# Token lists of the expert units built by small TensorE products instead of a scatter through DRAM; router constants built in steps; zeros of the output written later

## The chip, the core and the metric

The kernel runs on one core of a Trainium2 chip. The metric is device time in microseconds (us); lower is better. TensorE (PE), VectorE (DVE), ScalarE (ACT), GpSimd (POOL) and SyncE (SP, which only issues transfers here) each run their own queue in order; an instruction at the head of a queue holds everything behind it until the semaphores that it waits for are set.

## What is computed

Four batches of 576 tokens go through attention over 32 memories per head, then a gated MLP (512 to 1536 to 512), then a mixture of 8 experts with one expert per token and a capacity.

```python
a = exp(phi - max(phi, axis=2)); a /= sum(a, axis=2)            # per batch and head
k_m, v_m = einsum('bhsm,bhsd->bhmd', a, k), einsum('bhsm,bhsd->bhmd', a, v)
x = softmax(q @ k_m.T / 8) @ v_m                                # 2304 tokens x 512
x = (silu(x @ w_gate) * (x @ w_val)) @ w_out                    # 512 -> 1536 -> 512
expert = argmax(x @ moe2_w_gate); gate_w = softmax(...)[expert] # 8 experts
# tokens of an expert in order, at most `capacity`; others give 0
out[i] = gate_w[i] * (relu(x[i] @ w1[expert]) @ w2[expert])     # 512 -> 1024 -> 512
```

## The kernel before

All large products are float32 in three passes over rounded high and low parts (each operand is cut once: the high part by ACT at L370, the low part by DVE or POOL at L372). Weights arrive in 128x512 pieces, are turned by one ACT and three DVE instructions (L676 to L682), cut, used for the tokens of pass 1, stored to DRAM (`wsc`, `osc`) and loaded again at L730 for pass 2, which takes the second 1152 tokens.

Per batch, attention makes the memories (`kvp`, `tv`, L478 to L534) and the scores `at`; `pm` (L761) folds the memories into the gate and value weights, cut into `mh`; `pg` and `pv` (L863) are the gate and value products, 128x288 each; ACT makes `sg` (L773), DVE multiplies (L776), and the cut result `gh` enters `py` (L907, the MLP's output), summed over three groups G of the hidden width. Where the last group is done, `rows_out` adds up the rows (`rows`, L945), `store_rows` writes them to the DRAM tensor `x2` (L982), PE turns them (`pw`, L956) and multiplies by the router's weights `rg` (`pl`, L966).

`route` runs once for each of 6 blocks of 384 tokens. From the logits it finds each token's expert and its position in the expert's list (DVE instructions of 24 elements or less, four small PE products L1050 to L1054), and writes the token numbers with three indirect DMAs (L280, POOL) to the list tensor `perm` in DRAM. `weigh` stores the gate weights beside the rows (`gr`, L1115). `unit_table` turns the counts into units of 288 list places: two early ones, taken after pass 1's tokens, and six late ones. `unit_slots` lets SP read each unit's first place into a register and loads its 288 numbers (`idx`, L1212); `usable` makes `idg` of them (L1223, L1225). A unit then gathers its rows from `x2` (`xr`, L1301, POOL), turns them (`pxt`, L1324), multiplies by its expert's weights (`p`, L1351 and L1391), turns back (`po`, L1417) and scatters to the output (L280).

`routing_tables` builds the router's constants (`tri`, `rev`, `capf`, `thr`, `rg` and others) in one go: after batch 1's attention is done, all its instructions stand in one row on each engine, with three transfers (`cap_i`, `perm`, `rg32`). Then `tables` issues 18 writes of zeros to `x2` (second half) and 18 to the output (L1605).

What stands where in each engine's queue is settled when the kernel is built. A planner (`Loom`) steps through the work as threads: of those that could start on the engine that is free first it takes the one with the lowest rank (the table `RANK` shifts ranks), by assumed costs of each instruction (`on_v`, `on_a`, `on_pe`, `on_dma`). The result is a fixed order; nothing is moved at run time.

Of the kernel before, what the change touches and what calls it, by code (L numbers as in the profile page):

```python
# [20 lines left out]
RANK = {  # L21
    "gate": -9.6, "mh": 21.5, "mem": -52.9, "mem0": -65.1, "py": 200.6, "out": 236.4, "tables": 237.0, "warm": -9,
# [5 lines left out]
    "py1": 18.8, "turn": -10.4, "route": -70.2, "zeros": 4.5, "lists": -31.0, "reload": 13.3, "w1": 79.0, "w2": 46.2,  # L28
    "gather": 179.4, "x": 62.0, "up": 31.6, "hidden": -83.6, "down": 7.4,
    "l": (120.7, -0.9, 139.8, 37.0, 32.1, 45.2, 46.4, 56.0, 62.2, 66.5, 80.1, 63.5, 98.2, 102.9, 183.0, 198.1, 201.7, 200.6),  # L30
    "w": (-35.1, 193.1, 24.8, 183.1, 35.8, 36.6, -20.5, 2.0, 176.1, 45.2, 213.9, 197.4, 173.3, 173.5, -36.9, 103.7, 192.5, 95.3),
# [18 lines left out]
class Loom:  # L50
# [5 lines left out]
    def __init__(self, slack=0.0):  # L56
        self.slack, self.table = slack, AF.Exp
# [62 lines left out]

    def run(self):
        while self.ready:
            start, _, th = min(((max(t.time, self.busy[t.want[0]]), t.rank, t) for t in self.ready), key=lambda x: x[:2])
            start += self.slack
            th = min(
                (t for t in self.ready if t.want[0] == th.want[0] and max(t.time, self.busy[t.want[0]]) <= start),
                key=lambda t: (t.rank, max(t.time, self.busy[t.want[0]])),
# [4 lines left out]
            start = max(th.time, self.busy[engine])  # L132
# [7 lines left out]
            else:  # L140
# [3 lines left out]
                if engine == "V" and len(th.want) > 2 and self.busy["G"] > start:  # L144
                    cost += 0.45 * min(cost / 0.55, self.busy["G"] - start)
# [35 lines left out]
def on_swdge():  # L181
    return "G", 0.95


SWDGE_LANDING = 2.5
# [3 lines left out]
def attention_moe_moe_kernel(  # L189
# [35 lines left out]
    PADBASE = E * NT  # L225
    NPERM = 128 * ((PADBASE + NB + 127) // 128)
# [71 lines left out]
    onesb = tri = rev_i = rev = tokid = cap_i = capf = ej_i = ejf = thr = unit_val = trib = uio_i = uio = x2 = perm = mark = carry = cnt = rg = zero = undone = None  # L298

    def routing_tables():  # L300
        nonlocal onesb, tri, rev_i, rev, tokid, cap_i, capf, ej_i, ejf, thr, unit_val, trib, uio_i, uio, x2, perm, mark, carry, cnt, rg, zero, undone
        onesb = sb.tile([128, 128], BF16, name="onesb")
        nc.vector.memset(onesb, 1.0)
        tri = sb.tile([128, 128], BF16, name="tri")
        nc.gpsimd.affine_select(tri, onesb, [[1, 128]], ALU.is_gt, 0.0, base=0, channel_multiplier=-1)
# [528 lines left out]
    def batch(b):  # L834
# [38 lines left out]
        loom.put(b_s)  # L873

    rows_stored = {k: Event() for k in range(2 * NTC)}
    early_gathered, pls, pl_left = Event(), {}, {}

    def products(P):

# [838 lines left out]
```

## Time and profile before

| | us |
|---|---|
| median of 3 runs | 725.56 (724.23 to 727.99) |
| profiled execution | 721.09 |
| its span | 719.1 |
| PE busy in it | 658.3 |

PE works 92% of the span, so the time is PE's work and the gaps in it. Idle time of other engines costs nothing unless PE waits for it. A row of the timeline gives start and length, engine, line, operation, tiles, the number of like instructions, and in brackets how long the engine had been idle and whose end let it go on.

### The profile page before, as it was taken

To read this page: it belongs to the slowest core of one execution; us is meant where nothing else is said; L and a number is where in the kernel's file an instruction comes from. 1 tells how busy PE (TensorE), PEld (TensorE's weight loads), DVE (VectorE), ACT (ScalarE), POOL (GpSimd) and SP (SyncE) were. 2 spreads that over 40 slices of the span, in tenths; PEclk is the share of its full clock that TensorE was granted. 3 is DMA by queue.
4 is the path that set the end of the run, shared out by engine and by line. 5 is a ranking of instruction groups with operands and counts; after the bars stand their busy time and mean duration, and the time that the engine had idled before them with its cause. 6 is when DMAs were issued, how large, how long until landed. Compare 5 with 4: busy or idle time off the path is not lost. (4 is left out here: it accounts for less than half of the span.)

```text
span 719.1 us, 12573 instructions
## 1 busy us (share of the span) xinstructions
PE 658.3 (92%) x4656; PEld 604.7 (84%) x4656; DVE 440.9 (61%) x890; ACT 364.2 (51%) x693; POOL 247.8 (34%) x232
## 2 busy tenths in 40 slices
PE   2599879999997998999999999998999999999893
PEld 2488669887886987898998998897999999999892
DVE  3799956479999754732444465761763754853633
ACT  3567647666577723744642552533454543643531
POOL 2175543435444603533221230223542531430302
PEclk9889989999999999999999999999999999999997
DMA  9877699996594536392420432604857845645431
GB/s 360 319 278 268 217 286 243 317 356 221 208 379 155 205 118 125 98 225 89 177 99 35 147 118 103 118 2 146 274 158 213 254 123 206 211 155 171 149 119 35
DMA packets 56224, 134.49 MB, mean 187 GB/s; under 512 B 10399, under 2 KB 24351, under 8 KB 51552
## 3 DMA queue, kind: packets, MB, share of 16 engines
q1 hardware_dynamic: 52352, 123.91, 54.1%
q0 software_dynamic: 3808, 9.75, 4.3%
q8 instruction: 38, 0.62, 0.4%
q14 instruction: 26, 0.21, 0.1%
HBM read 98.11 MB, written 35.79 MB: 186 GB/s over the span
## 5 line engine op out<-in xcount | busy, mean ns | idle before, releaser
L907 PE MATMUL py<-wo,gh 128*128 128x512 f32 x648 | 156.6, 393 | 0.8 <-POOL wo L372 0.8
L907 PEld LDWEIGHTS py<-wo,gh 128*128 128x128 f32 x648 | 118.9, 188 | 24.9 <-POOL wo L372 1.2
L372 POOL TENSOR_TENSOR gh<-sg,gh 128x288 fp32r<-128x288 f32 x96 | 84.3, 884 | 133.5 <-ACT gh L370 133.5
L1391 PE MATMUL p<-hh,w2h 128*128 128x288 f32 x768 | 115.6, 302 | 0.4 <-DVE xt L372 0.4
L1351 PE MATMUL p<-xt,w1h 128*128 128x288 f32 x768 | 112.6, 299 | 1.0 <-DVE ohb L1040 0.6
L1391 PEld LDWEIGHTS p<-hh,w2h 128*128 128x128 f32 x768 | 106.2, 191 | 1.0 <-DVE xt L372 0.6
L1351 PEld LDWEIGHTS p<-xt,w1h 128*128 128x128 f32 x768 | 105.4, 191 | 1.4 <-DVE ohb L1040 0.8
L863 PE MATMUL pg<-at,mh 128*128 128x288 f32 x576 | 97.3, 303 | 9.3 <-DVE mh L372 3.5
L863 PE MATMUL pv<-at,mh 128*128 128x288 f32 x576 | 93.3, 299 | 4.7 <-ACT sg L773 4.7
L863 PEld LDWEIGHTS pg<-at,mh 128*128 128x128 f32 x576 | 83.6, 191 | 16.6 <-DVE mh L372 5.7
L280 POOL DMA_INDIRECT out_dram<-ot,idx x24 | 48.9, 2038 | 134.7 <-DVE ot L1430 130.5
L863 PEld LDWEIGHTS pv<-at,mh 128*128 128x128 f32 x576 | 82.1, 190 | 5.9 <-ACT sg L773 5.0
L372 DVE TENSOR_TENSOR mh<-pm,mh 64x512 fp32r<-64x512 f32 (+1 forms) x88 | 60.3, 685 | 14.4 <-ACT mh L370 12.6
L776 DVE SCALAR_TENSOR_TENSOR sg<-sg,pv 128x288 f32<-128x288 f32 x96 | 42.5, 448 | 40.9 <-PE pv L863 24.5
L1365 ACT ACTIVATE hh<-p 128x288 fp32r<-128x288 f32 x64 | 26.2, 409 | 74.4 <-PE p L1351 72.2
L1367 DVE SCALAR_TENSOR_TENSOR hh<-p,hh 128x288 fp32r<-128x288 f32 x64 | 28.7, 450 | 53.4 <-ACT hh L1365 53.4
L370 ACT ACTIVATE gh<-sg 128x288 fp32r<-128x288 f32 x96 | 41.9, 442 | 36.4 <-DVE sg L776 35.5
L370 ACT ACTIVATE mh<-pm 64x512 fp32r<-64x512 f32 (+1 forms) x88 | 51.9, 590 | 13.2 <-PE pm L761 5.1
L372 DVE TENSOR_TENSOR w2h<-w2r,w2h 128x1024 fp32r<-128x1024 f32 x36 | 43.6, 1214 | 20.9 <-ACT w2h L370 20.9
L372 DVE TENSOR_TENSOR w1h<-w1r,w1h 128x1024 fp32r<-128x1024 f32 x36 | 43.1, 1219 | 20.9 <-PE pv L863 11.6
L761 PE MATMUL pm<-wgv,tv 128*128 128x256 f32 x336 | 48.5, 294 | 7.6 <-ACT wgv L370 6.0
L761 PEld LDWEIGHTS pm<-wgv,tv 128*128 128x128 f32 x336 | 45.1, 200 | 9.3 <-ACT wgv L370 6.3
(192 smaller groups left out, 839.8 us busy)
## 6 DMA issues: line engine op xcount, KB each, us to landing
w1r<-in_moe_w_dram SPq DMA_DIRECT2D x36, 512.0 KB, 4.8
w2r<-in_moe_w_dram SPq DMA_DIRECT2D x36, 512.0 KB, 5.2
wr<-in_moe_w_gv_dram SPq DMA_DIRECT2D x24, 512.0 KB, 6.4
wsc<-wgv SPq DMA_DIRECT2D x12, 1024.0 KB, 6.1
wgv<-wsc SPq DMA_DIRECT2D x12, 1024.0 KB, 7.1
kvraw<-in_kv_dram SPq DMA_DIRECT2D x16, 640.0 KB, 7.2
wr<-in_moe_w_out_dram SPq DMA_DIRECT2D x12, 512.0 KB, 6.6
osc<-wo SPq DMA_DIRECT2D x6, 1024.0 KB, 4.9
```

The lines of the kernel that those rows point to most:

```text
L280: ins = nc.gpsimd.indirect_dma_start(*args, **kwargs)
L370: nc.scalar.activation(hi, src, AF.Copy)
L372: (nc.gpsimd if pool else nc.vector).tensor_sub(lo, src, hi.bitcast(F32))
L761: nc.tensor.matmul(pm[:, Q * 256 : (Q + 1) * 256], tv[:, 2 * Q + hp, a, :], w[:, c, 2 * Q + hp], start=(k == 0 and n3 == 0), stop=(k == le ...
L776: nc.vector.scalar_tensor_tensor(sg, sg, 2.0**-16, pv[:, :NB], ALU.mult, ALU.mult)
L863: nc.tensor.matmul(pg[:, :NB], mh[:, a, Q, gv * 128 : gv * 128 + 128], at[:, Q, c, ns], start=(Q == 0 and n3 == 0), stop=(Q == 1 and n3 == 2),
L907: nc.tensor.matmul(py, gh[:, a, k * TC : (k + 1) * TC], wtiles[P, ws[j // 2]][:, j % 2, c, :], start=(j == 0 and n3 == 0), stop=(j == FG - ...
L1351: nc.tensor.matmul(p1[:, :NB], self.w1[d][:, a, f * 128 : f * 128 + 128], self.xt[d][:, c], start=(d == 0 and n3 == 0), stop=(d == NDT - 1 ...
L1365: nc.scalar.activation(dst[:, 0], p1[:, :NB], AF.Relu)
L1367: nc.vector.scalar_tensor_tensor(dst[:, 1], p1[:, :NB], 0.0, dst[:, 0].bitcast(F32), ALU.max, ALU.subtract)
L1391: nc.tensor.matmul(p2[:, :NB], self.w2[f // 2][:, f % 2, a, d * 128 : d * 128 + 128], self.hh[f][:, c], start=(f == 0 and n3 == 0), stop=( ...
```

## The change

Line numbers of the kernel after are higher: L372 is L429 there, L863 is L920, L907 is L964, L730 is L787, L1324 is L1453, L1351 is L1480, L1391 is L1520, L1417 is L1546, L1301 is L1432.

**Lists.** `perm`, its 18 scatters and the register reads are gone. `route` keeps for each token its place modulo 96 (`places`) and a group number for each third of a unit (`groups`). `marks` writes a 0/1 matrix `ones` (token by place) with one DVE comparison of 128x288 per block; `slots` writes `picked` (token by unit and third, times the token's number in two digits) with DVE, and sums ones x picked over 128-token blocks on PE: 9 products for the early units, 18 for the late ones. Six DVE instructions turn the sum into `idg` and `idx`. The last, small unit copies its column with four short transfers.

**Constants.** They are made in single steps from the moment that batch 0's scores start, each step ranked by the planner. **Zeros.** `x2` is not zeroed any more (early gathers read its first half only); the output's 18 zero writes wait until pass 2's first group has let go of its weights. **Planner.** New ranks throughout; transfers are not issued over 40 us ahead of the modelled DMA; POOL's work is charged to DVE where both run.

```diff
-    "gate": -9.6, "mh": 21.5, "mem": -52.9, "mem0": -65.1, "py": 200.6, "out": 236.4, "tables": 237.0, "warm": -9,
+    "gate": -427.7, "mh": -121.7, "mem": -6.5, "mem0": -3.9, "py": 225.9, "out": 216.2, "tables": 206.8, "warm": -9,
...
+    def tables():
...
+        yield atts[0].phq[0]
+        yield on_dma(20)
         nc.sync.dma_start(cap_i, capacity.bitcast(I32)[0:1].partition_broadcast(128))
+        yield on_dma(60)
+        nc.sync.dma_start(rg32, r_gate.rearrange("(t p) e -> p t e", p=128))
...
+            yield on_v(80)
+            nc.vector.tensor_copy(dst, src)
...
+    def zeros():
+
+        yield listed
+        yield wfree[1, (0,)]
+        for i in range(NT // 128):
+            yield on_dma(262)
+            nc.sync.dma_start(
...
@@ route @@
-        for c in range(RB):
-            yield on_swdge()
-            scatter(
-                "perm",
...
+        over = small([TC, RB, NQ - 1], "over", BF16)
+        yield on_v(69)
+        nc.vector.tensor_tensor(
...
+        nc.vector.tensor_reduce(q96, over, AX.X, ALU.add)
...
@@ lists @@
-        nc.sync.dma_start(idx[:, i], perm[bass.ds(first, NB)].rearrange("(p c) one -> p (c one)", c=NC))
...
+    def marks(key):
...
+        for blk in range(NBLK // 2 if early else NBLK):
             yield placed[blk]
+            yield on_v(RB * CH)
+            nc.vector.tensor_tensor(
+                t[:, blk * RB * CH : (blk + 1) * RB * CH].rearrange("p (t s) -> p t s", s=CH),
...
+    def slots(key, n, firsts, pk, left):
...
+        for a in range(2):
+            yield on_v(T * w)
+            nc.vector.tensor_tensor(
+                picked[:, :, a], picked[:, :, 1], number[:, :T, a : a + 1].to_broadcast([128, T, w]), ALU.mult
+            )
+        pt = pk[:CH, 128 : 128 + 2 * w]
+        yield on_pe(T, 100)
+        for i in range(T):
+            nc.tensor.matmul(
+                pt, ones[:, i], picked[:, i].rearrange("p a w -> p (a w)"), start=(i == 0), stop=(i == T - 1)
+            )
...
@@ tables @@
-        yield NEXT + RANK["zeros"]
-        for i in range(NT // 256, NT // 128):
-            yield on_dma(262)
-            nc.sync.dma_start(
-                x2[i * 128 : (i + 1) * 128, :DM].rearrange("p (t c) -> p t c", t=NDT),
-                zero.unsqueeze(1).to_broadcast([128, NDT, 128]),
-            )
...
```

SP at the start of the program, before (`wr` raw weights, `kvraw` keys and values, `ph` phi, `qt` queries):

```order
L439 DMA qt<-in_q_dram 128x1152 x2
L666 DMA wr<-in_moe_w_gv_dram 128x1024 x2
L416 DMA kvraw<-in_kv_dram 128x1280 x2
L396 DMA ph<-in_phi_dram 128x576 x2
L439 DMA qt<-in_q_dram 128x1152
L416 DMA kvraw<-in_kv_dram 128x1280 x2
```

And after:

```order
L723 DMA wr<-in_moe_w_gv_dram 128x1024 x2
L453 DMA ph<-in_phi_dram 128x576 x2
L473 DMA kvraw<-in_kv_dram 128x1280 x2
L496 DMA qt<-in_q_dram 128x1152
L453 DMA ph<-in_phi_dram 128x576 x2
L473 DMA kvraw<-in_kv_dram 128x1280 x2
```

Weights, phi and keys now come ahead of the queries; `cap_i` and `rg` (the router's weights) follow eight transfers later, ahead of the seventh piece of weights.

DVE where the constants are made, before (`wr` and `mag` are weights being turned, `sg` the gate times the value):

```order
L678 TENSOR_SCALAR wr_906<-mag_982 128x512
L494 RECIPROCAL rs_1026<-rs_1026 128x1
L303 MEMSET onesb_1066 128x128
L309 CAST rev_1072<-rev_i_1070 128x8
L315 CAST capf_1078<-cap_i_1076 128x1
L320 TENSOR_SCALAR ej_i_1080<-ej_i_1080 64x1
```

And after:

```order
L833 SCALAR_TENSOR_TENSOR sg_521<-sg_521,pv_504 128x288
L369 CAST shift_82<-ints_176 128x3
L429 TENSOR_TENSOR mh_522<-pm_442,mh_522 128x512
L369 CAST uio_89<-ints_176 64x16
L557 TENSOR_TENSOR kvs_529<-kvp_326,rh_513 128x2x2x64
L369 CAST capf_83<-cap_i_117 128x1
L739 SCALAR_TENSOR_TENSOR mag_456<-mag_456,wr_352 128x512
L833 SCALAR_TENSOR_TENSOR sg_550<-sg_550,pv_538 128x288
```

The 17 rows that stood together before are 22 single rows among the first gates' work now.

PE in the two early units, where the late lists are made, before (`hh` and `w2h`: second product, `y2` turned back):

```order
L1417 MATMUL po_5513<-ident_63,y2_5202 96x128
L1417 MATMUL po_5514<-ident_63,y2_5202 96x128
L1417 MATMUL po_5515<-ident_63,y2_5202 96x128
L1391 MATMUL p2_5556<-hh_5146,w2h_4702 128x288 x6
L1391 MATMUL p2_5556<-hh_5146,w2h_4752 128x288 x6
```

And after:

```order
L1546 MATMUL po_5469<-ident_63,y2_5187 96x128
L1546 MATMUL po_5470<-ident_63,y2_5187 96x128
L1546 MATMUL po_5471<-ident_63,y2_5187 96x128
L1520 MATMUL p2_5504<-hh_5130,w2h_4686 128x288 x6
L1520 MATMUL p2_5504<-hh_5130,w2h_4735 128x288 x6
L1318 LDWEIGHTS ones_5049
L1318 MATMUL pk_5381<-ones_5049 96x42
```

The 18 list products stand in a row there, each with its weight load; the first late gather's `pxt` comes 21 rows of large products behind the last of them.

## Rows read from the trace of the kernel before

**Rows 1.** Page, parts 1 and 2: busy time; granted clock in 40 slices.

```profile
PE 658.3 (92%) x4656; PEld 604.7 (84%) x4656; DVE 440.9 (61%) x890; ACT 364.2 (51%) x693; POOL 247.8 (34%) x232
...
PEclk9889989999999999999999999999999999999997
```

**Rows 2.** Waits of PE by line: us in total, times, longest us.

```profile
PE pg L863 <- DVE mh L372: 3.5, 4, 1.9
PE pxt L1324 <- DMA xr<-x,idg: 3.1, 3, 2.4
```

**Rows 3.** Stretches: busy PE, PEld, DVE, ACT, POOL, granted clock, DMA share, GB/s.

```profile
40.00:60.00 20.00, 19.91 (x196) 18.10 (x196) 19.69 (x36) 13.78 (x30) 14.82 (x13) 0.96 0.81 280
...
160.00:180.00 20.00, 17.82 (x97) 14.59 (x96) 19.84 (x32) 12.24 (x23) 11.56 (x10) 1.00 0.67 225
...
480.00:500.00 20.00, 18.18 (x138) 17.93 (x137) 2.29 (x7) 6.92 (x13) 3.57 (x4) 1.00 0.32 100
```

**Rows 4.** Timeline of PE at the start.

```profile
36.16 0.58 PE L761 MATMUL pm<-wgv,tv 128*128 128x256 f32 x1 [6.02 <-ACT wgv L370]
...
44.43 1.06 PE L863 MATMUL pg<-at,mh 128*128 128x288 f32 x6
```

**Rows 5.** Timeline, 94 to 112: PE, then ACT, DVE and SP.

```profile
105.67 1.81 PE L863 MATMUL pv<-at,mh 128*128 128x288 f32 x6 [4.72 <-ACT sg L773]
...
109.94 0.95 PE L863 MATMUL pv<-at,mh 128*128 128x288 f32 x6
...
104.60 0.22 ACT L357 CAST rg<-rg 128x32 fp32r<-128x32 f32 x1 [6.17 <-DMA rg<-in_moe_w_gate_dram]
...
104.08 0.15 DVE L315 CAST capf<-cap_i 128x1 f32<-128x1 int32 x1 [4.99 <-DMA cap_i<-in_moe_capacity_dram]
...
99.99 0.42 SPq L356 DMA_DIRECT2D rg<-in_moe_w_gate_dram  x1
```

**Rows 6.** Timeline, 278 to 290: PE, then DVE.

```profile
279.01 0.17 PE L1052 MATMUL pl<-ohb,onesb 128*128 128x16 bf16 x1
279.03 0.17 PE L1053 MATMUL pl<-ohb,onesb 128*128 128x8 bf16 x1
...
283.19 0.66 PE L956 MATMUL pw<-ident,rows 128*128 128x128 f32 x4 [2.44 <-DVE rows L945]
...
282.44 0.69 DVE L945 TENSOR_TENSOR rows<-py,yp 128x512 f32<-128x512 f32 x1 [4.02 <-DMA x<-rows]
```

**Rows 7.** Transfers of 262 to 290, then 420 to 458: KB, us to landing.

```profile
x<-rows SPq DMA_DIRECT2D x5, 256.0 KB, 8.9
...
perm<-tokid,addr POOLq DMA_INDIRECT x6, 12.0
x<-gr SPq DMA_DIRECT2D x2, 6.0 KB, 10.0
...
x<-rows SPq DMA_DIRECT2D x9, 256.0 KB, 2.3
```

**Rows 8.** Timeline, 470 to 506: PE, then DVE and SP.

```profile
475.78 3.48 PE L1391 MATMUL p<-hh,w2h 128*128 128x288 f32 x24
...
500.61 0.27 PE L1324 MATMUL pxt<-ident,xr 96*128 96x96 f32 x1 [2.43 <-DMA xr<-x,idg]
...
502.56 3.25 PE L1351 MATMUL p<-xt,w1h 128*128 128x288 f32 x12 [0.35 <-DVE hh L1367]
...
477.05 3.50 DVE L372 TENSOR_TENSOR w1h<-w1r,w1h 128x1024 fp32r<-128x1024 f32 x3
...
494.33 0.17 DVE L1223 TENSOR_SCALAR valid<-idx 96x18 f32<-96x18 int32 x1 [7.05 <-DMA idx<-perm]
...
486.34 5.73 SPq L1212 DMA_DIRECT2D idx<-perm  x6
```

**Rows 9.** Timeline of SP: zeros of the output; reloads of output weights.

```profile
128.62 12.62 SPq L1605 DMA_DIRECT2D out_dram<-zero  x13
...
395.56 4.43 SPq L730 DMA_DIRECT2D wo<-osc  x2
```

More of the change, by code (lines that the diff above doesn't have):

```diff
@@ L21 @@
 RANK = {
-    "gate": -9.6, "mh": 21.5, "mem": -52.9, "mem0": -65.1, "py": 200.6, "out": 236.4, "tables": 237.0, "warm": -9,
[5 rows of a table removed]
[L28 to L31, printed above, removed]
+    "gate": -427.7, "mh": -121.7, "mem": -6.5, "mem0": -3.9, "py": 225.9, "out": 216.2, "tables": 206.8, "warm": -9,
[5 rows of a table added]
+    "mh1": -125.4, "py1": 5.2, "turn": -32.0, "route": -35.0, "zeros": -96.4, "lists": -142.7, "marks": -35.9, "pick": 100.3,
[3 rows of a table added]
 }
@@ L119, in put, with earliest @@
             slots.free.append(self.now + self.hop())
+    def earliest(self, th):
+        time = max(th.time, self.busy[th.want[0]])
+        return max(time, self.busy["DMA"] - self.look) if th.want[0] == "SP" and len(th.want) == 2 else time
     def run(self):
         while self.ready:
-            start, _, th = min(((max(t.time, self.busy[t.want[0]]), t.rank, t) for t in self.ready), key=lambda x: x[:2])
+            start, _, th = min(((self.earliest(t), t.rank, t) for t in self.ready), key=lambda x: x[:2])
             start += self.slack
             th = min(
-                (t for t in self.ready if t.want[0] == th.want[0] and max(t.time, self.busy[t.want[0]]) <= start),
-                key=lambda t: (t.rank, max(t.time, self.busy[t.want[0]])),
+                (t for t in self.ready if t.want[0] == th.want[0] and self.earliest(t) <= start),
+                key=lambda t: (t.rank, self.earliest(t)),
             )
@@ L131, in run @@
             self.running = engine
-            start = max(th.time, self.busy[engine])
+            start = self.earliest(th)
             if engine == "SP" and len(th.want) > 2:
@@ L143, in run @@
                     cost += 1.3
-                if engine == "V" and len(th.want) > 2 and self.busy["G"] > start:
-                    cost += 0.45 * min(cost / 0.55, self.busy["G"] - start)
+                if engine == "V" and len(th.want) > 2:
+                    if self.busy["G"] > start:
+                        cost += 0.45 * min(cost / 0.55, self.busy["G"] - start)
+                    self.shared = start + cost
+                if engine == "G" and self.shared > start:
+                    self.busy["V"] += 0.45 * min(cost, self.shared - start)
                 self.busy[engine] = th.time = start + cost
@@ new lines, in tables @@
+        for dst, src in (
+            (place_of, parts[0]),
+            (steps, parts[1]),
+            (number[:, :, 0], parts[2]),
+            (number[:, :, 1], parts[3]),
+            (rev[:, 0, :], parts[4]),
+            (shift, parts[5]),
+            (uio, parts[6][:NEJ]),
+            (capf, cap_i),
+        ):
+            yield on_v(80)
+            nc.vector.tensor_copy(dst, src)
+        ej = ints[:NEJ, at : at + 2]
+        yield on_v(40)
+        nc.vector.tensor_scalar(ej[:, 0:1], parts[7][:NEJ], 3, None, ALU.arith_shift_right)
@@ L1190, in unit_table @@
[L1190 to L1193 removed]
+        nc.vector.tensor_copy(tab, tabf[:, 0:17])
         tabs[early] = tab
         loom.set(tab_ready[early], loom.now + 0.3)
[L1198 to L1202 removed]
+        if not early:
+            yield on_v(16)
+            nc.vector.tensor_copy(firstf, pk[:, 64:80])
@@ L1203, in unit_slots @@
+        left[0] -= 1
+        if not left[0]:
+            loom.put(banks)
+    idxs, idx_ready, turned_on = {}, {key: Event() for key in "eld"}, {}
+    marked = {key: Event() for key in "eld"}
+    def marks(key):
+        early = key == "e"
+        yield placed[0 if early else NBLK // 2]
+        yield raw_s
+        turned_on[key] = t = traw([128, 2560], "ones", BF16)
         for blk in range(NBLK // 2 if early else NBLK):
             yield placed[blk]
-        n, tab, key = len(us), tabs[early], "d" if dyn is not None else "e" if early else "l"
@@ L1469, in gather @@
             yield landed
[L1470 removed]
+            self.idx = idx
             yield self.prev.got
```

316 lines of the change are left out of this document (183 added, 133 removed), and 13 rows, old and new, of the table RANK.

## The prediction

> **What bounds the kernel now.** I read the busy times first. PE works 658.3 of 719.1 us [rows 1], so 60.8 us are gaps, and some work is stretched: the granted clock is 10 tenths in most slices, 7 to 9 in a few. I then took 20 us stretches one by one. Most of those after 300 us are full. In 40 to 60 and 160 to 180 VectorE is busy 19.69 and 19.84 of 20 us [rows 3], and the PE gaps there wait for `mh`, which VectorE cuts: 3.5 us over four waits [rows 2]. That part of the kernel is bound by VectorE's order, and small things put among its work count there. The list of waits by line then gives single long gaps, and the timeline at each of them tells who came last. Four concern the change.
>
> Start: `pm` waits 6.02 us for the cut of the first weights and the first `pg` starts at 44.43 [rows 4].
>
> Constants: VectorE and ScalarE both stand, 4.99 and 6.17 us, at the head of their queues, for `cap_i` and for `rg`, issued at 99.99; behind them stand a cut of `mh` and the gates. PE starts `pv` at 105.67 after 4.72 idle, and the six products then last 1.81 us instead of 0.95 [rows 5]: the clock has gone to half (1.2 of 2.4 GHz) after the gap.
>
> Rows: VectorE stands 4.02 us at `rows` for the store of older rows that must leave their buffer, and PE's `pw` comes 2.44 us late [rows 6].
>
> Lists: `valid` stands 7.05 us until SP has read the six lists back, issued from 486.34 on one behind another in 5.73 us; the gathers follow it, and `pxt` waits at 500.61 [rows 8], in three waits for 3.1 us in all [rows 2].
>
> **The change part by part**, against the profiled execution of 721.09 us.
>
> *Constants in steps.* The transfers go out behind the first weights and queries, tens of us before their first use. Both stalls go, and with them `pv`'s 4.72. From 105.67 to 109.94 stand 18 products (12 of 128x288, 6 of 128x256) in 4.27 us; at 0.145 or less each (24 in 3.48, [rows 8]) they take 2.6 at most, so 1.7 to 2 of clock go too. Together 6.6. What is late next there: the cut of `mh` and the gates that stood behind the two waits, and their inputs were ready. The instructions do not vanish: 22 small ones at about 0.15 [rows 5] are 3.3 us at most, less where they overlap the tails of others, and they now stand in VectorE's bound stretch after 40 us. Seventeen of them cost nothing before, being under the stall. I charge 1.5, between 0 and 3.3.
>
> *Start.* The queries go behind weights, phi and keys. The sixth weight piece still ends the wait for `pm`, but phi's sums and the keys' products are no longer behind the weights. Counting the VectorE work ahead of the first `pg` I expect it 2 to 4 us before 44.43; I take 3, less the 1.5 above: 1.5 net. The bounds are -2 and 4.5.
>
> *Scatters gone.* In 262 to 290 the six scatters took 12.0 us (median) from issue to landing, and stores of rows among them 8.9; with no scatters around, in 420 to 458, the same stores took 2.3 [rows 7]. With 2.3 the store that held `rows` would land over 6 us sooner, so the 4.02 go. PE gets back 2.44 and a clock dip. Its price I take from the dip after the lists: 12 products in 3.25 us instead of 1.74, so 1.5 [rows 8]. Together 3.9; bounds 0 and 3.9.
>
> The Trainium skill has a rule for this ("DMA: Bandwidth & Descriptors", section "Queues, rings and completion order"): a transfer's semaphore is a strongly ordered write that lands only after every earlier write from that engine, across its queues. By that rule a store that moves fast still signals late behind a slow scatter, which the 8.9 against 2.3 agrees with. It would hold as well behind the `gr` store, which stays: by that reading none of the 3.9 comes back.
>
> *Lists on chip.* The chain was: last scatter, its landing, six reads in turn, landing, `valid`, gather. Now it is VectorE and PE work. The route gets four more small instructions (0.6 us); the last mark of 128x288 costs 0.35, estimated from `w1h`'s 1.17 for 1024 columns [rows 8]; the picks of 18 blocks by 42 columns, by the same price per column, some 3.5; 18 products; four small instructions, 0.7. Three `w1h` cuts, 3.50, lie on the way [rows 8]. The choice of units is made some 3 us ahead of the cuts that start at 477.05 [rows 8]; from there the sum of these pieces ends at 484 to 487 instead of 494.5. VectorE has only 2.29 us of work in 480 to 500 [rows 3], so nothing else delays it. PE comes to the list products at an estimated 484.5 (by their place in the order, some 9 us of products behind 475.78 [rows 8]), so it may wait up to 2 us there; the gathers then land some 8 us sooner than before, against the 3.1 that they were late. Gone: 3.1, the following 0.35, and 1.5 of clock: 5.0. Bounds: 2 (a new wait of 2 us with a dip at the products) and 5.0.
>
> The products themselves: 27, each with a weight load of 128x96. The nearest rows are the router's bf16 products, 0.17 us long but 0.02 apart [rows 6]; with loads I take 0.06, so 1.6 us lost, bounds 0.5 and 4.6. The marks (nine at 0.35) and the extra route work (0.6 in each of six blocks) fall in 260 to 480, where VectorE is the waiting engine; PE's work covers them. If it did not, they would cost at most 6.8 together. GpSimd loses 18 scatters and SP its reads, and nobody waits for the gain beyond what is counted.
>
> *Zeros later.* In the old place nobody on PE waited for them. In the new one they stand on SP ahead of the reload of `wo` for the next group. Thirteen took SP 12.62 us [rows 9], so 18 take 17.5; a reload then needs 4.4 or so for two [rows 9] and lands perhaps 5 us after issue: 22 to 25 us. PE's cover, by the order of the kernel after, is 156 products of 128x288, 24 of 128x256 and six of 128x512 between the last use of the old tile and the first of the new: 25 to 27 us at 0.133 to 0.145 each. It just fits. I charge 0.5, bounds 0 and 4.5 (3 late and a dip).
>
> *New ranks.* Every order in the first 240 us is another one. The stretches of 20 us from 40 to 240, of which two have 0.09 and 2.18 us of gap [rows 3], add up to some 10 us without the constants' stall, and that can shrink or grow. From about 510 us on the order of PE is that of before, and the tail does not move. I take 0, bounds -6 and +6.
>
> **Sum:** -6.6 - 1.5 - 3.9 - 5.0 + 1.6 + 0.5 = -14.9. Some short waits at the logits (below 1 us each) should go with the faster stores: -15.5 in all. The profiled execution would be 705.6. The median of the runs shown is 4.5 above the profiled execution, so on that footing the forecast is 725.6 - 15.5 = 710.
>
> **Rivals.**
>
> *The row stores stay late.* The 16-byte pieces of `gr` hold the queue, not the scatters: `gr` itself took 10.0 us [rows 7]. For it: it is issued among the same stores. Against it: the store that held `rows` was issued before it. Then 3.9 stay: 714.
>
> *VectorE eats it.* In its bound stretches the 22 constants and the new order delay each gate a little, as the 19.69 and 19.84 of 20 allow [rows 3]. The start gains nothing and the order costs 6: 1.5 and 6 off the gain, 717.5. Against it: the constants' stall is a single late transfer, which no order of small instructions brings back.
>
> *The reload comes late.* Zeros slower than 12.62 for 13, or a tile freed late: 3 us and a dip, and the following groups' gate weights wait behind it too: up to 6, so 716.
>
> *It does not do what it says: the list still ends last.* If the picks end after 497, where PE would reach `pxt`, nothing of the 5.0 comes, and the products add: 715.
>
> *Slower than before.* The new ranks put weight cuts ahead of the gates while VectorE is full, and PE waits at gate after gate from 40 to 240 us. The point from which it decides is 26 us of gaps there instead of some 10; at 31 us it would give 731. Against it: the summed VectorE work ahead of the first gates grows by 1 to 3 us only, by the order.
>
> **How the numbers follow.** Half a percent, 3.6 us, is about what a measurement of this kernel tells from no change: faster means under 721.9, slower over 729.2. The forecast (703 to 713 with its small terms) has 0.60; rows late 0.11; VectorE 0.14; reload 0.05; lists 0.05; slower 0.05, of which some ends within the half percent. Of the VectorE case a quarter is worse than its price and ends as no change. That gives faster 0.88, same 0.08, slower 0.04. The low end of the range, 701, is the forecast with the start at its best bound and the order 6 better; the high end, 719, holds the rivals except the tail of the VectorE case and the slower one.
>
> **What would show it.** Right: no VectorE wait for `cap_i`, no half clock at about 100 us, row stores of 2 to 3 us at 270, no `pxt` wait, PE full from 480 to 510. Wrong: a PE wait for `pg` or `pv` in 40 to 100 longer than before; `rows` still waiting for stores; PE standing at the list products for VectorE; a wait of `py` for the reloaded `wo`; more gaps in 160 to 240. The prediction fails most easily at the order of the first 240 us, which I could only bound.

## The result and the profile after

| | before | after |
|---|---|---|
| median of the runs on one chip, us | 725.98 (724.23 to 727.99, 4 runs) | 703.99 (702.52 to 709.66, 4 runs) |
| profiled execution, us | 721.09 | 702.52 |
| its span, us | 719.1 | 700.7 |

The ratio of the runs is 0.971, with a 95% interval of 0.965 to 0.977. The medians are 22 us apart, the profiled executions 18.6. The forecast was 15.5 off and 710; its range held the time. The traces can explain 18.6. The other 3 us come from the other runs: those of before lie 3 to 7 us above its profiled one, those of after 1, 2 and 7 above theirs. I have no trace of them.

Busy time and granted clock in the page of the kernel after, against [rows 1]: PE is busy 4 us less although 25 products were added. The sixth slice (90 to 108 us before, 88 to 105 now), with 8 tenths before, has 9 now; the fifth (70 to 88) has fallen from 9 to 8, behind two waits for `wo`, and the second from 8 to 6, where `pm` waits 9.0 in place of 6.02.

```profile
PE 653.9 (93%) x4681; PEld 600.6 (86%) x4681; DVE 455.6 (65%) x948; ACT 366.2 (52%) x695; POOL 237.0 (34%) x217
...
PEclk9689899999999999999999999999999999999998
```

PE's waits in the kernel after (us in total, times, longest). Gone against [rows 2]: `pxt` for its gather, and all but 0.5 of `pg` for `mh`. Grown: `pm`, and `po` for `y`, the turned output on ScalarE (2.4 over two waits before). `pw` still waits for `rows`, at other places: VectorE's `rows` waits there for PE's `py` and no longer for a store. New: `pk` for the lists' small inputs; and 2.6 at 23 us for the queries, now behind weights, phi and keys; that wait lies ahead of the longer one of `pm`.

```profile
PE pm L818 <- ACT wgv L427: 9.0, 1, 9.0
...
PE po L1546 <- ACT y L1535: 3.0, 3, 1.6
PE pw L1013 <- DVE rows L1002: 2.8, 3, 1.6
PE py L964 <- POOL wo L429: 2.4, 2, 1.6
...
PE pk L1246 <- DVE self_f L1244: 1.6, 2, 0.8
```

Where the time came from is read from landmarks: products that stand in both kernels, and when each starts. Here are two of them on PE's timeline, the early and the late units' products of `kinds` (which expert gets a unit), before:

```profile
299.96 0.19 PE L1136 MATMUL pk<-kinds,trib 64*64 64x1 bf16 x1 [0.21 <-DVE kinds L1134]
...
472.03 0.19 PE L1155 MATMUL pk<-kinds,trib 64*64 64x2 bf16 x1
```

and after, with the first gate, the list products, the first late gather and a `po` near the end:

```profile
42.07 0.96 PE L920 MATMUL pg<-at,mh 128*128 128x288 f32 x6
...
289.60 0.19 PE L1200 MATMUL pk<-kinds,trib 64*64 64x1 bf16 x1
...
462.21 0.19 PE L1219 MATMUL pk<-kinds,trib 64*64 64x2 bf16 x1
...
466.54 0.17 PE L1246 MATMUL pk<-self_f,onesb 64*128 64x16 bf16 x1 [0.74 <-DVE self_f L1244]
...
472.85 0.95 PE L1318 MATMUL pk<-ones 128*96 128x42 bf16 x18
...
484.75 0.53 PE L1546 MATMUL po<-ident,y 128*96 128x128 f32 x3 [0.96 <-ACT y L1535]
486.75 0.41 PE L1453 MATMUL pxt<-ident,xr 96*128 96x96 f32 x3
...
667.89 0.53 PE L1546 MATMUL po<-ident,y 128*96 128x128 f32 x3 [1.60 <-ACT y L1535]
668.18 3.44 PE L1520 MATMUL p<-hh,w2h 128*128 128x288 f32 x24
```

The same last two rows before:

```profile
683.39 0.88 PE L1417 MATMUL po<-ident,y 128*96 128x128 f32 x3 [2.08 <-ACT y L1406]
683.92 4.68 PE L1391 MATMUL p<-hh,w2h 128*128 128x288 f32 x24
```

The start of the same product does not mean the same work done, because the orders differ. Ahead of the early `kinds`, `pg` and `pv` have 702 products before and 738 after (PE's busy time and, in brackets, products of their line up to the landmark; before, then after):

```profile
0.00:299.96 299.96, 108.35 (x702) 0.97 0.74 245
0.00:289.60 289.60, 108.46 (x738) 0.96 0.64 233
```

Ahead of the late `kinds`, the units' first products `p` have 72 before and 96 after:

```profile
0.00:472.03 472.03, 11.04 (x72) 0.98 0.63 201
0.00:462.21 462.21, 14.32 (x96) 0.97 0.57 200
```

Back to back, 36 such products take 4.76 us (603.30 to 608.06 in the kernel after), 0.132 each. So at equal work the kernel after is further ahead than the starts say: 4.8 at the early `kinds`, 3.2 at the late ones. At the first late `pxt` it is 1.6 less ahead (12 products fewer), and at the first `pg` 1.3 less (20 products of `kvp` fewer, priced by e1's row below). From the `po` near the end on the work is the same.

| landmark | before | after | ahead | ahead at equal work | forecast: terms that lie before it |
|---|---|---|---|---|---|
| first `pg` | 44.43 | 42.07 | 2.4 | 1.1 | start: 3, less part of 1.5 |
| early `kinds` | 299.96 | 289.60 | 10.4 | 15.1 | constants 6.6, start 1.5, rows 3.9: 12.0 |
| late `kinds` | 472.03 | 462.21 | 9.8 | 13.0 | the same, zeros -0.5: 11.5 |
| first late `pxt` | 500.61 | 486.75 | 13.9 | 12.3 | lists 3.1 of 5.0, products -1.6: 13.0 |
| `po` near the end | 683.39 | 667.89 | 15.5 | 15.5 | rest of the lists: 14.9 |
| last products | 705.32 | 688.27 | 17.0 | 17.0 | tail 0: 14.9 |
| end of the span | 719.1 | 700.7 | 18.4 | 18.4 | 14.9 (15.5 with small waits) |

At equal work, then: 3.1 more than forecast by 300 us, 1.6 less between the two `kinds`, 0.9 less over the late lists (2.5 for 3.4), and 2.9 of tail that I had taken as unchanged. The experiments show part of what stands behind the first of these: the constants' 6.6 came through only because the zeros moved, which I had charged as a loss, and the new ranks, which I had put at nothing, gave several us.

### The profile page after: what moved, and what is told of

The parts are those of the page before. It is cut to its first block, busy times and chain, and to the rows that moved or that the text cites. A ratio compares the mean times of both kernels' runs of the same rounds, so it can differ in the third digit from the quotient of the medians.

```text
span 700.7 us, 12589 instructions
## 1 busy us (share of the span) xinstructions
PE 653.9 (93%) x4681; PEld 600.6 (86%) x4681; DVE 455.6 (65%) x948; ACT 366.2 (52%) x695; POOL 237.0 (34%) x217
## 5 line engine op out<-in xcount | busy, mean ns | idle before, releaser
L964 PE MATMUL py<-wo,gh 128*128 128x512 f32 x648 | 157.0, 396 | 2.4 <-POOL wo L429 2.4
L964 PEld LDWEIGHTS py<-wo,gh 128*128 128x128 f32 x648 | 120.4, 190 | 27.0 <-POOL wo L429 3.2
L429 POOL TENSOR_TENSOR gh<-sg,gh 128x288 fp32r<-128x288 f32 x96 | 84.3, 885 | 170.7 <-ACT gh L427 165.7
L1520 PE MATMUL p<-hh,w2h 128*128 128x288 f32 x768 | 113.3, 299 | 0.2 <-issue 0.2
L1480 PE MATMUL p<-xt,w1h 128*128 128x288 f32 x768 | 110.6, 297 | 0.6 <-DVE xt L429 0.6
L1520 PEld LDWEIGHTS p<-hh,w2h 128*128 128x128 f32 x768 | 104.3, 189 | 0.5 <-ACT xt L427 0.3
L1480 PEld LDWEIGHTS p<-xt,w1h 128*128 128x128 f32 x768 | 104.0, 189 | 0.9 <-DVE xt L429 0.8
L287 POOL DMA_INDIRECT out_dram<-ot,idx x24 | 54.4, 2265 | 131.0 <-DVE ot L1559 127.9
L920 PE MATMUL pg<-at,mh 128*128 128x288 f32 x576 | 95.7, 301 | 2.0 <-POOL at L429 0.7
L920 PE MATMUL pv<-at,mh 128*128 128x288 f32 x576 | 92.9, 298 | 0.0
L920 PEld LDWEIGHTS pg<-at,mh 128*128 128x128 f32 x576 | 82.3, 190 | 6.9 <-DVE mh L429 2.0
L920 PEld LDWEIGHTS pv<-at,mh 128*128 128x128 f32 x576 | 82.2, 190 | 0.8 <-issue 0.4
L429 DVE TENSOR_TENSOR mh<-pm,mh 64x512 fp32r<-64x512 f32 (+1 forms) x88 | 60.3, 685 | 24.7 <-ACT mh L427 22.8
L429 DVE TENSOR_TENSOR w2h<-w2r,w2h 128x1024 fp32r<-128x1024 f32 x36 | 43.6, 1216 | 21.7 <-ACT w2h L427 21.7
L1432 POOL DMA_INDIRECT xr<-x,idg x24 | 27.0, 1123 | 73.1 <-DVE idx L1343 64.0
```

The source lines that it names most:

```text
L287: ins = nc.gpsimd.indirect_dma_start(*args, **kwargs)
L429: (nc.gpsimd if pool else nc.vector).tensor_sub(lo, src, hi.bitcast(F32))
L920: nc.tensor.matmul(pg[:, :NB], mh[:, a, Q, gv * 128 : gv * 128 + 128], at[:, Q, c, ns], start=(Q == 0 and n3 == 0), stop=(Q == 1 and n3 == 2),
L964: nc.tensor.matmul(py, gh[:, a, k * TC : (k + 1) * TC], wtiles[P, ws[j // 2]][:, j % 2, c, :], start=(j == 0 and n3 == 0), stop=(j == FG - ...
L1432: nc.gpsimd.indirect_dma_start(self.xr[:, c], None, x2[: NT // 2] if self.early else x2, bass.IndirectOffsetOnAxis(idg[:, c : c + 1], 0))
L1480: nc.tensor.matmul(p1[:, :NB], self.w1[d][:, a, f * 128 : f * 128 + 128], self.xt[d][:, c], start=(d == 0 and n3 == 0), stop=(d == NDT - 1 ...
```

## Experiments

Each ratio is to runs of the kernel before on the same chip. The chips differ: its median was 725.0 for e1 to e4, 729.9 for e5 to e8 and 729.0 for e9 to e12.

**e1, constants alone.** In the kernel before, the two transfers go out behind the sixth piece of weights (in the kernel after they stand just ahead of it, at 15.06 and 16.61):

```
-        nc.sync.dma_start(cap_i, capacity.bitcast(I32)[0:1].partition_broadcast(128))
+        cap_i = early_loads["cap_i"]
...
+        if early_loads["n"] == 6:
+            nc.sync.dma_start(early_loads["cap_i"], ...)
+            nc.sync.dma_start(early_loads["rg32"], ...)
```

> The kernel before with one change: cap_i and the router's weights are loaded right behind the sixth weight load (the start) instead of at about 100 us. Everything else, the block of constants on VectorE included, stands where it stood. Theory (one late transfer makes the whole stall): VectorE and ScalarE do not wait at 98 to 104 us, PE's gap of 4.72 before pv and the half clock until 109.9 are gone, 6.6 us less, about 719 against 725.5. Rival (VectorE's order takes the gain, since the 17 small instructions still run ahead of the gates and something else is late next): 3 us or less, 722.5 or more.

Measured: 719.73, ratio 0.9937 [0.9904, 0.9969], 4.6 us, between theory and rival. The stall of [rows 5] is gone, and two waits stand behind it, in PE's timeline:

```profile
104.23 0.80 PE L868 MATMUL pg<-at,mh 128*128 128x288 f32 x4 [1.95 <-DVE mh L371]
...
148.40 1.29 PE L477 MATMUL kvp<-kvraw,ex 112*32 112x128 f32 x20 [2.10 <-DMA kvraw<-in_kv_dram]
```

The second is behind SP's zeros: the raw keys `kvraw` are issued only after them.

```profile
127.15 12.27 SPq L1610 DMA_DIRECT2D out_dram<-zero  x13
...
140.44 3.24 SPq L415 DMA_DIRECT2D kvraw<-in_kv_dram  x2
```

The first is behind a cast of two columns that lasted 2.35 us on VectorE, most of them while GpSimd ran two instructions with two inputs; it ended when they did, at 102.0 (VectorE, then GpSimd):

```profile
99.68 2.35 DVE L323 CAST ejf<-ej_i 64x2 f32<-64x2 int32 x1
...
99.97 0.79 POOL L371 TENSOR_TENSOR gh<-sg,gh 128x288 fp32r<-128x288 f32 x1
100.73 1.28 POOL L371 TENSOR_TENSOR wgv<-mag,wgv 128x512 fp32r<-128x512 f32 x1
```

By the late `kinds` nothing of e1's gain is left (472.79 against 472.03, with the same order of PE). The 2.9 us by which its span is shorter come behind them, where e1 changes nothing.

**e5, the same without the zeros of `x2` and of the output:**

> The kernel before with the constants' transfers early (as e1_const_early) and without all zero writes (left out: the zeros of the output and of the second half of x2; early gathers read the first half). In e1_const_early PE got 4.6 to 5.3 us back and then waited 2.1 us at 146 for keys that stand behind the zeros on SP. Theory (the zeros in their old place take back part of the constants' gain): that wait goes, 2 to 3 us less than e1_const_early, about 717. Rival (the zeros cost nobody anything): within 1 us of e1_const_early, 719 to 720.

Measured: 724.31, ratio 0.993 [0.9896, 0.9965], no better than e1. By the time alone the rival holds. A landmark says more. Here is a product that stands at the same place in these kernels, the scores `psc` behind the gates, and ahead of it the first gate; before (its first gate at 44.43 is in [rows 4]),

```profile
164.54 1.19 PE L565 MATMUL psc<-qt,tk 128*64 128x288 f32 x8
```

in e1,

```profile
44.45 1.07 PE L868 MATMUL pg<-at,mh 128*128 128x288 f32 x6
...
163.08 1.19 PE L564 MATMUL psc<-qt,tk 128*64 128x288 f32 x8
```

and in e5:

```profile
43.06 1.07 PE L868 MATMUL pg<-at,mh 128*128 128x288 f32 x6
...
156.94 1.19 PE L564 MATMUL psc<-qt,tk 128*64 128x288 f32 x8
```

From the first gate to the scores before took 120.1 us, e1 118.6 and e5 113.9. Constants alone are worth 1.5 there; with the zeros out of the way 6.2. (The first gate itself differs by 1.4 between executions of the same start, so it is taken off. PE's order is the same in the three.) e5 has the late cast too, with the same 1.95 at 102.80; from there on the zeros make all of the difference, 4.7. Of these, waits for keys are 2.3 (2.10 and 0.19), and a wait of `pg` for `mh` at 160 us, 1.65 in e1 and 0.45 in e5, is 1.2; the rest I cannot place. The wait for `mh` stands in the kernel before too (1.64 at 161.95), so up to 1.2 might have come from the zeros alone; no run takes them alone out of the kernel before. By the early `kinds` 3.9 of e5's 6.2 are left, and more is lost later, in longer waits than in the kernel after: `hh` 5.9, `rows` 3.9 and `y` 3.5. Just ahead of the first, VectorE stood 9.12 us until 481.12 for something that the trace gives only as "remote".

**e2 and e3, scatters or `gr`.** The kernel before without the token numbers' scatters of pass 1, and without the `gr` stores of pass 1 (e3 writes zeros there instead, with nine small writes more in SP's block of zeros at 100 us):

```
             yield on_swdge()
+            if blk < NBLK // 2:
+                continue
             scatter(
                 "perm",
```

> The kernel before without the nine scatters of token numbers of the first three blocks (left out: the numbers of pass 1's tokens, so that the early units write nothing and the late lists miss these tokens); the stores of gate weights (gr) stay. Theory (slow scatters hold back the signal of the row stores): row stores issued at 268 to 276 land in 2 to 4 us instead of 9 to 10, VectorE's 4.0 us at rows and PE's 2.4 at pw go with the clock dip: 3.9 us less. Rival (the 16-byte pieces of gr hold them): the row stores still take 8 to 10 us, time within 1 us of before.

```
+        if blk >= NBLK // 2:
             nc.sync.dma_start(x2[blk * RB * TC : (blk + 1) * RB * TC, DM:].rearrange("(c p) r -> p c r", p=TC), gr)
```

> The kernel before without the stores of gate weights of the first three blocks (left out: pass 1's gate weights, which are zeros instead, written at 100 us with the other zeros); the scatters stay. Theory (scatters): row stores at 268 to 276 still land in 8 to 10 us, VectorE still waits 4 us at rows, time within 1 us of before. Rival (gr): the wait goes and 3.9 us with it.

Measured: e2 718.07, ratio 0.9901 [0.9867, 0.9935]; e3 728.68, ratio 1.0044 [1.0021, 1.0067]. Transfers of e2 in 262 to 290, KB and us to landing, against [rows 7]: row stores land in 2.6 instead of 8.9 and `gr` itself in 2.1 instead of 10.0. (These are medians of few: the two stores issued among the scatters took 10.0 and 8.9 before, the one ahead of them 2.3; in e2 the known ones took 2.8 and 2.3.)

```profile
x<-rows SPq DMA_DIRECT2D x4, 256.0 KB, 2.6
x<-gr SPq DMA_DIRECT2D x2, 6.0 KB, 2.1
```

PE's waits in e3 still have the late rows, and the one row store behind its scatters whose landing is known (issued at 286.71) took 12.7:

```profile
PE pw L956 <- DVE rows L945: 4.1, 1, 4.1
...
DMA to landing us min/median/max: 12.7/12.7/12.7
```

So the scatters hold the stores, and the rival with `gr` falls. That e3 is 3.7 us slower than before is not explained; its stalls at the constants (6.2) and at `pw` (4.1) are longer than those of [rows 5] and [rows 6]. From the first product of the logits (`pl<-yh,rg`, 245.38 before and 243.18 in e2) to the early `kinds` (299.96 and 293.51) before took 54.6 us and e2 50.3: 4.3 less, where I had priced 3.9. The rule that the prediction quoted (the Trainium skill, "DMA: Bandwidth & Descriptors", section "Queues, rings and completion order") agrees for the scatters; whether the stores moved late or only signalled late, no run tells. `gr`, which e2 keeps, held nothing back by itself.

**e4 and e6, the ranks.** The kernel before with the new ranks and planner's rules, then the same with e5's constants and no zeros. (The 1.5 us for an output scatter that the text of e4 names is not in these kernels: they plan it at 0.95.)

```
-    "gate": -9.6, "mh": 21.5, "mem": -52.9, ...
+    "gate": -427.7, "mh": -121.7, "mem": -6.5, ...
```

> The kernel before with the ranks and the planner's rules of the kernel after (limit of 40 us on early transfers, POOL's work charged to VectorE, 1.5 us for an output scatter); lists by scatter and constants in one block as before. Theory (the gaps of 120 to 240, some 11 us before and 6 after, are the order's; the stalls are the lists' and the constants'): those gaps fall by about 5, the start by 2, the waits for cap_i, for rows and for the lists are still there in some form: 3 to 8 us less, 717 to 722. Rival (all of the gain beyond the forecast comes from lists and constants, and the order alone gives nothing): 725 or more, gaps of 120 to 240 as before.

> The kernel before with the new ranks and planner's rules, the constants' transfers early and no zero writes; lists still by scatter through DRAM (left out: the zeros as in e5). In e4_order_alone PE stood 9.0 us at 142 for weights that ScalarE got 5 us late, behind 14 zero writes. Theory (new order and old transfers clash, the order itself is good): the 9.0 and the 2.9 before it go, and what is left against the kernel after is the lists' and rows' stalls of 5 to 8 us: 709 to 714. Rival (the order itself is bad without the new lists): over 725.

Measured: e4 746.74, ratio 1.0283 [1.0241, 1.0324]; e6 748.88, ratio 1.0242 [1.0159, 1.0326]. In e4 PE waits for weights at 150.80, since ScalarE waits for the raw ones, which SP issues behind 14 zeros (PE, ACT, SP):

```profile
150.80 0.58 PE L769 MATMUL pm<-wgv,tv 128*128 128x256 f32 x1 [8.96 <-ACT wgv L378]
...
143.23 0.66 ACT L684 ACTIVATE mag<-wr 128x512 f32<-128x512 f32 x1 [5.10 <-DMA wr<-in_moe_w_gv_dram]
...
123.45 14.26 SPq L1613 DMA_DIRECT2D out_dram<-zero  x14
137.81 1.62 SPq L674 DMA_DIRECT2D wr<-in_moe_w_gv_dram  x2
```

Removing zeros and stall in e6 did not mend it. This wait of `pm` falls from 8.96 to 4.4 there, but 7.8 for `hh` at 498 and shorter waits stand in its place. Both theories fell, and both times lie in the rivals' ranges. The new ranks cost 21 us in the kernel before (e4) and 25 with early constants and no zeros (e6 against e5, on one chip), without the new lists and single-step constants.

**e7, the kernel after with the old ranks** (the two ranks that are new, for marks and picks, and the planner's rules kept from after, its look-ahead widened to 100 us):

> The kernel after with the ranks of before (its new threads marks and pick keep theirs) and no limit on early transfers. Theory (the stalls' removal is most of the gain, the order 5 to 8 us): constants 6.6, rows 3.9, lists 2 to 5 less than before: 709 to 714. Rival (the order carries the gain): 718 or more.

Measured: 722.49, ratio 0.9847 [0.9768, 0.9926], faster than before by 11 us by the ratio and 7 by the medians; its four runs lie between 716.8 and 728.1. The theory (709 to 714) fell, and the time lies in the rival's range: without the ranks and the 40 us limit the kernel after loses some 10 (by the ratios) to 15 (by the medians) of its 22. The same ranks cost 21 in the kernel before: they belong to one set of work and have no price of their own.

**e8, the kernel after with the 18 zeros early**, in one piece from 131.24 on:

```
+        if loads["n"] == 23:
+            for i in range(NT // 128):
+                nc.sync.dma_start(out[...], zero...)
```

> The kernel after with its 18 zero writes issued in one piece at about 122 us, behind the 23rd raw weight load, instead of at 324 to 341; all orders else the same. Theory (in the stretch where weights and keys are loaded the zeros push them back): loads behind are 10 to 15 us late, PE waits for keys or cut weights near 140 to 150, 4 to 10 us more: 708 to 714. Rival (any place is as good, the queues have room): within 1 us of the kernel after, 703 to 705.

Measured: 720.82, ratio 0.9872 [0.9797, 0.9948]. PE's timeline shows one wait of 13.59 that the kernel after does not have, for keys issued behind the zeros:

```profile
157.76 2.51 PE L532 MATMUL kvp<-kvraw,ex 112*32 112x128 f32 x28 [13.59 <-DMA kvraw<-in_kv_dram]
```

The late `kinds` start 14.9 us later than after's (477.14 against 462.21, in the same order of PE), 13.5 counted from the first gate. The theory holds, with a price above the 4 to 10 expected.

**e12, the kernel after without zeros at all:**

> The kernel after without the 18 writes of zeros to the output; the output is not cleared, nothing else is left out. Theory (in the new place nobody on PE waits for them or for the reload of wo behind them): within 1.5 us of the kernel after, ratio 0.969 to 0.973. Rival (the zeros at 324 to 340 us still hold the reloads and row stores of the group that follows): 2 to 5 us faster than the kernel after, ratio 0.964 to 0.968, with shorter PE waits between 330 and 400.

Measured: 704.21, ratio 0.9653 [0.9612, 0.9694]. The ratio alone would speak for the rival, but runs of before were 3 us slower on this chip; the time is that of the kernel after. The trace decides: from the early to the late `kinds` e12 takes 172.60 us (289.65 to 462.25) and the kernel after 172.61, and in 320 to 400 PE is as busy with the zeros as without. One stretch of the kernel after,

```profile
320.00:340.00 20.00, 20.00 (x151) 19.48 (x150) 11.14 (x23) 12.78 (x26) 7.76 (x9) 1.00 0.83 240
```

and the same of e12:

```profile
320.00:340.00 20.00, 20.00 (x151) 19.47 (x151) 11.10 (x23) 12.78 (x26) 7.72 (x9) 1.00 0.45 153
```

Only the DMA share differs. In the new place the zeros cost nothing.

**e9 and e10, the constants' small instructions.** In e9 each stands twice; in e10 ScalarE makes the eight casts:

```
             nc.vector.tensor_copy(dst, src)
+            nc.vector.tensor_copy(dst, src)
```

> The kernel after with each of the 20 small VectorE instructions of the constants (casts, thresholds, memsets) written twice in a row: the same values, the same order otherwise. Theory (they are real work on an engine that is the late one from 46 to 100 us, some 4 us of busy time in the trace of the kernel after, above the 1.5 that the prediction charged): 1.5 to 4 us slower than the kernel after, ratio to before 0.973 to 0.977, and the waits of PE for mh and of pv for ScalarE's tv grow in 46 to 100. Rival (they fit into VectorE's gaps): within 1 us of the kernel after, ratio near 0.971, with the waits of 46 to 100 as they are there.

```
-            nc.vector.tensor_copy(dst, src)
+            nc.scalar.copy(dst, src)
```

> The kernel after with the eight casts of the constants made by ScalarE in place of VectorE, at the same places of the program. Theory (three of the casts last 0.8 us on VectorE, and only where they overlap GpSimd's instructions with two inputs, against 0.13 to 0.17 elsewhere; VectorE is the late engine there): VectorE gets about 3 us back, and the kernel gets 0.5 to 2 us faster than the kernel after, ratio 0.968 to 0.971. Rival (ScalarE has as little room there, since a copy costs it more than a cast costs VectorE and pv waits for its tv): 0 to 3 us slower than the kernel after, with longer PE waits for ACT in 40 to 100.

Measured: e9 710.72, ratio 0.9734 [0.9689, 0.9779]; e10 703.90, ratio 0.9662 [0.962, 0.9704]. e9 is 6.5 to 8.3 us slower than its three neighbours on the chip. Part is there at once: `pt` waits 3.82 for VectorE's `kvs` at 63.57, 0.82 in after, and the early `kinds` are 4.1 late. Of this, 1.5 stand already at `pm` (35.45 against 33.99), ahead of the first doubled instruction, but only 0.4 at the first `pg` (42.51 against 42.07). Another 4.2 come behind the late `kinds`, where nothing was doubled; there a wait for `y` was followed by half clock, which the one at this place in the kernel after was not:

```profile
674.63 0.73 PE L1556 MATMUL po<-ident,y 128*96 128x128 f32 x3 [2.15 <-ACT y L1545]
675.02 4.92 PE L1530 MATMUL p<-hh,w2h 128*128 128x288 f32 x24
```

In e10 the early `kinds` start at 287.94, 1.7 us sooner than in after, and VectorE's busy time in 40 to 60 falls from 19.25 to 16.44. The end of the last products is 0.4 sooner only; `po` waits 4.2 for `y` instead of 3.0. In this one trace the gain is there at 300 us and is given back later.

**e11, `y` ahead of the weight cuts.** The planner is told that unit weights land 2.5 us later, which lets it put `y` first on ScalarE:

```
-                loom.spawn(self.part1(d, raw), self.base - 8 + d + RANK["w1"], loom.landed)
+                loom.spawn(self.part1(d, raw), self.base - 8 + d + RANK["w1"], loom.landed + 2.5)
```

> The kernel after, with the planner told that each unit's weights land 2.5 us later than it assumes. It changes no work; it lets the planner put the turned outputs y ahead of the cuts of w1h, behind whose transfers they stand on ScalarE at 484, 540 and 666 us. Theory (the small waits of po for y, 3.0 us in the trace of the kernel after, are a matter of which instruction stands first on ScalarE): these waits fall under 1 us, and the kernel is 1 to 3 us faster than the kernel after, ratio 0.967 to 0.970. Rival (the cuts that now come later hold the products of the next unit): p waits for w1h in place of po for y, same time or up to 4 us slower, ratio 0.971 to 0.977.

Measured: 702.40, ratio 0.9636 [0.9593, 0.9679]. The waits for `y` fall from 3.0 to 0.9 as expected, and the one at 668 goes. In their place comes a wait for the gather of the small unit, and half a clock behind it:

```profile
588.23 0.98 PE L1618 MATMUL pxt<-ident,xr 128*128 128x128 f32 x4 [3.51 <-DMA xr<-x,idg_s]
588.86 3.14 PE L1520 MATMUL p<-hh,w2h 128*128 128x288 f32 x12
```

Neither e10 nor e11 is shown to beat the kernel after: their intervals overlap its own, and their times are within 2 us of it, on another chip.

## Why the prediction came out right, step by step

**Constants: the 6.6 was about right, "their inputs were ready" was not.** e5 has 6.2 at 164 us, of which up to 1.2 may be the zeros' own. But I named only the gates as late next. e1 shows others, a cast held up by GpSimd and the transfers behind the zeros, and the zeros took 4.7 of the 6.2. This step alone was worth 1.5 at 164 us and nothing at 470.

**Zeros: wrong sign.** "In the old place nobody on PE waited for them" was true, but for 1.2 at `mh`, only as long as PE was late itself. I charged 0.5 for the move. It cost nothing in the new place (e12), as "it just fits" said, and it is what lets the constants' gain through; in the kernel after, undoing it costs 12 us by the ratios (e8). The step that failed: I asked what the zeros would hold in the new place, and not what they would hold in the old one once the stall ahead of them was gone.

**Scatters: right,** in mechanism and size: 3.9 forecast, 4.3 in e2. One reading was loose: 420 to 458 is not free of scatters, three go out from 449.36 on, and the row store of 455.45 behind them took 8.3. The 2.3 is the size of those ahead of them.

**Start: right in sign, smaller.** This pair of traces shows 2.4, but it is a lucky pair. The first `pg` stands at 43.06 to 44.45 in the five traces with the old start (before, e1, e2, e3, e5) and at 42.07 to 43.46 in the six with the new one; the means are 0.95 apart. 1.5 net was forecast, and 20 products of `kvp` are put off behind it.

**Small constants: undersized.** 1.5 charged, 3.3 as a bound at 0.15 each. Three casts (`rev`, `uio`, `ejf`) lasted 0.8, each under an instruction of GpSimd with two inputs. DVE in the kernel after,

```profile
46.54 0.80 DVE L369 CAST rev<-ints 128x8 f32<-128x8 int32 x1
49.47 0.15 DVE L369 CAST shift<-ints 128x3 f32<-128x3 int32 x1
50.14 0.80 DVE L369 CAST uio<-ints 64x16 f32<-64x16 int32 x1
```

and GpSimd at the same time:

```profile
46.50 0.82 POOL L429 TENSOR_TENSOR gh<-sg,gh 128x288 fp32r<-128x288 f32 x1 [1.55 <-ACT gh L427]
...
50.10 0.81 POOL L429 TENSOR_TENSOR gh<-sg,gh 128x288 fp32r<-128x288 f32 x1 [1.54 <-ACT gh L427]
```

Both `gh` end with the cast, at 47.3 and 50.9; the casts beside them, with no such instruction on GpSimd, take 0.13 to 0.20. e9 puts the price of the set at 2.6 to 3.6 us by 300 (4.1 less the 1.5 at `pm` or the 0.4 at the first `pg`), above my charge and about at its bound.

**New ranks: 0 was wrong.** By 300 us the parts add to 6.2 (e5, of which 3.9 are left there), 4.3 (e2) and 2.4 of start, less 2.6 (e9): 10.3 at most. At equal work the kernel after is 15.1 ahead. So about 5 are left for the new order, and e7 puts ranks and look-ahead at 10 to 15 for the whole kernel, beyond my bound of 6; e4 gives +21 for the same table in the kernel before. I took it as a part that could be worth 6 either way, and it is one that fits one set of work or the other. These sums set terms from single executions side by side, so 1 or 2 us can hide in them.

That the forecast of 710 held is therefore in part luck: with the old ranks the other parts gave 7 to 11 (e7), where I had added up 13 without the start, and the ranks made up for it. My chances were also added up loosely: by their own parts "faster" is 0.92 and not 0.88.

**Lists: right in mechanism, smaller.** The wait of `pxt` is gone with no new one at the products. From the late `kinds` to `pxt` 28.6 us became 24.5, but in the new order `pxt` has 36 products fewer ahead of it there, 4.8 us of work; so nothing was gained up to `pxt`. From the late `kinds` to the `po` at 668, with equal work, the kernel gained 2.5, where the forecast had 5.0 less 1.6. The 18 products took 0.95, 0.053 each, near the 0.06 I took. Waits of 0.74 for `self_f`, 0.39 for `ones` and 0.96 for `y` came in place of that of `pxt`. Between the two `kinds` PE is idle 2.4 us instead of 0.8; 0.84 of this is the early lists' wait for `self_f` at 292.42, and their nine products take 0.4. No run has the lists alone.

**Tail: not unchanged.** The wait for `y` ahead of the last units was 2.08 before and 1.60 after. The first was followed by 24 products in 4.68 us, the second by 24 in 3.44. With the last write, which landed 1.3 us sooner after its issue, the tail gave 3.4 of the 18.4. Nothing in the change aims at it. From this `po` to the end five traces with the order of before take 34.1 to 35.8 us (before 35.7), and the kernel after, e8, e9, e10 and e12 take 32.8 to 34.6 (after 32.8). Before is near the top of its group and after at the bottom of its own, so I count most of this part of the gain as luck.

**Open.** Why the medians differ by 3 us more than the traces; what "remote" in e5 and in e3 (8.1 us on ScalarE at 494) stands for; what the lists are worth alone; and why the new ranks fail without the new lists.

## What to carry to other kernels

When a stall at the head of a queue goes, ask what else becomes late at that point, also a transfer that nobody waited for: here writes of zeros held back 4.7 of 6.2 us. Compare kernels by when the same product starts, since a part's gain seen at 160 us can be gone at 480 and a median shows only the rest. Where the order changed, count first what stands ahead of that product in each kernel: here 36 products more hid 4.8 us of gain. A table of ranks made for one set of work has no price of its own, so test the parts with either table.

## What the runs showed of the hardware

A cast of 8 columns took 0.80 us instead of 0.15 while GpSimd ran an instruction with two inputs, and one of two columns 2.35 where two such stood in a row. In e9 four casts of 0.60 to 1.49 ended within 0.1 us of such an instruction. It is not casts alone: in the kernel after `rh`, two columns, took 1.33 until `wgv` ended at 48.6 (VectorE, then GpSimd):

```profile
47.26 1.33 DVE L554 TENSOR_SCALAR rh<-bd,rs 128x2 f32<-128x2 f32 x1
...
47.27 1.30 POOL L429 TENSOR_TENSOR wgv<-mag,wgv 128x512 fp32r<-128x512 f32 x1
```

Beside GpSimd's iotas, which read nothing, a cast of 8 columns took 0.17 (before, 98.91). The Trainium skill ("SBUF — State Buffer", section "SBUF: two separate sides") has it as an exclusive lock on a pair of ports that VectorE and GpSimd share, held for the whole instruction; on VectorE's side it names instructions in a two-port mode or with two inputs from SBUF. The ends at 47.3 and 50.9 agree; which mode the casts ran in, no trace shows. On ScalarE eight of the casts took 0.19 to 0.26 (e10).

The half clock behind a wait is not told by the wait alone. At the `po` ahead of the last units, the products behind waits of 1.97 (e3), 2.08 (before), 2.15 (e9), 2.40 (e12), 2.72 (e8) and 3.13 us (e2) ran with a granted clock of 0.50, 1.2 GHz, and the 24 took 1.2 to 1.5 us more. Behind waits of 1.60 (after), 1.77 (e1), 2.30 (e5) and 2.73 (e10) at the same place it was 1.00, 2.4 GHz. In e10:

```profile
667.55 0.53 PE L1546 MATMUL po<-ident,y 128*96 128x128 f32 x3 [2.73 <-ACT y L1535]
667.84 3.42 PE L1520 MATMUL p<-hh,w2h 128*128 128x288 f32 x24
```

In the prediction each late wait carried 1.5 of clock as if it were certain.

Scatters of 4-byte token numbers, six within 28 us, made two neighbouring stores of 256 KB land in 8.9 and 10.0 us instead of 2.3 to 2.8, though GpSimd issued the scatters and SP the stores.
